# Loading four parameter arrays in 32-column pieces and turning them on VectorE, with a planner told of longer parameter loads

## The chip, the cores and the metric

One core of one Trainium2 chip runs the whole program. The metric is the device time of one execution in microseconds, the median of the runs taken. Engine names are those of the profile: PE is TensorE's matmul stream and PEld its weight loads, DVE is VectorE, ACT is ScalarE, POOL is GpSimd, SP is SyncE, which here only issues DMAs. Everything is float32; the two big matmuls of the MLP split each operand into a high and a low part and run in the `float32r` form.

## The reference

```python
xn = layernorm(u)                                  # u: 2048 tokens x 576 channels
dt = exp(log_dt)                                   # per channel
A  = -exp(log_A_real) + 1j * A_imag                # 576 x 128
C  = (C_real + 1j * C_imag) * dt[:, None]
K  = 2 * einsum("dn,dnl->dl", C, exp(A * dt[:, None] * pos)).real
y  = irfft(rfft(xn.T, 2L) * rfft(K, 2L))[:, :L].T  # a long convolution for each channel
s  = y + xn * D_skip
m  = gelu(layernorm(xn) @ w1 + b1) @ w2 + b2       # 576 -> 4608 -> 576, for each token
out = u + s * silu(m)
```

The four arrays of 576 x 128 that the change is about are `log_A_real`, `A_imag`, `C_real` and `C_imag`. The kernel wants them with the 128 modes on the partitions and the 576 channels along the free dimension, so each has to be transposed.

## The kernel before

**Two strands on one TensorE.** The MLP fills TensorE from start to end. It runs as 48 slots: two halves of the tokens, in each half 12 groups of 384 hidden units, and for each group two blocks of 512 tokens. A slot first makes three hidden tiles (`layer1`, L508: 14 matmuls of 512 columns each), then adds their products into four output tiles (`layer2`, L565: 72 matmuls of 288 columns). Between the two stand ACT (L541 gelu, L544 the high part `hh`) and DVE (L547, the low part `hl`). DVE also adds each finished output tile into `acc` (L573), and ACT and DVE split the next group's weights (L488, L485) as they arrive in the tile `raw` (L448, L450, L453, on SP's queue).

The convolution runs between the MLP's matmuls. Its parameters are prepared once (`params`, L664 to L776, the part that the change touches) and stored in DRAM in eight packs (`par_s`). For each of 36 blocks of 16 channels `tables` (L794) then loads a piece of them (`load_par`, L785, on POOL's queue, two buffers), makes sines and exponentials on DVE and ACT (first step L803 on DVE), and `kgen` (L872) multiplies them on TensorE (L885) into the convolution kernel. For each of six chunks of 96 channels `chunk` (L917) does the transforms: a forward stage (L958), a second stage (L996), the inverse (L1049) and a last stage (L1076), with DVE turning 32 x 32 blocks between them (L945, L1060). POOL stores the results (`s_s`, L1087). At half time the normalized tokens of the second half come back in pieces of 128 bytes (L1244) and DVE turns them (L1249).

**Who sets the order.** Every engine runs its instructions in the order in which they are written, and that order comes from a planner (`Order`, L55). It keeps a clock for each engine, gives each step a reckoned duration and, where it has one, a due time, and writes the step that can begin first. The strands are lists of steps; a step on `None` is a transfer: its loads are issued there, and what needs them is placed no sooner than its reckoned length later. The reckoned lengths of the convolution's TensorE stages are `X1, S2, INV, I1, KG` (L915). Two more numbers steer it: `END` (L1369), by which the stages of the chunks are spread over the run, and `ALONE` (L1370), how long a ready `kgen` waits for another convolution stage on which it can ride (`ride`, L896, then both are one interruption of the MLP) before it is written by itself.

**The parameters.** `loads` (L678) issues on SP's queue `log_dt`, and for each of the four arrays two DMAs, 512 rows and 64 rows, with 512 bytes to a packet. TensorE turns an array by four transposes of 128 x 128 and one of 64 x 128 (L692, L693) into PSUM (a pair of banks `cv`, which the convolution's stages use too), and ACT or DVE reads it from there. The tile names `kt`, `pr` and `mg` in the profile are the buffers of the raw arrays here: `kt` for `log_A_real` and `A_imag`, `pr` for `C_real`, `mg` for `C_imag`. The tile `U` holds `dt`. The rows behind these loads on SP's queue are the rest of the second group's `raw` weights (L450, L453), two small loads of `tvals` (L264), and eight loads of token rows (L346, tiles `w` and `v`), on which DVE takes the layer norm's statistics (L371).

Of the kernel before, what the change touches and what calls it, by code (L numbers as in the profile page):

```python
# [12 lines left out]
AF = mybir.ActivationFunctionType  # L13
OP = mybir.AluOpType
# [3 lines left out]
L, D, N, F = 2048, 576, 128, 4608  # L18
P = 128
# [3 lines left out]
CH = 96  # L23
# [10 lines left out]
PK = 72  # L34
# [4 lines left out]
TB = 512  # L39
# [168 lines left out]
def step(eng, dur, fn, need=(), mark=None, cv=0, at=0.0, late=0.0, tbl=None, by=1e9):  # L208
    return dict(eng=eng, dur=dur, fn=fn, need=tuple(need), mark=mark, cv=cv, at=at, late=late, tbl=tbl, by=by)
# [3 lines left out]
def mixer_kernel(ctx, tc, u, log_a_real, a_imag, c_real, c_imag, log_dt, d_skip, w1, b1, w2, b2,  # L213
                 f1, f2, g2, g1, tvals, ident, out, parts=("mlp", "s4d")):
    nc = tc.nc
# [34 lines left out]
    idt = ys_tile().rearrange("p i a b c -> p (i a b c)")[:, :P]  # L250
# [241 lines left out]
    turn = [0]  # L492
# [171 lines left out]
    def params():  # L664

        nrm, th, ph = (A2F[:, k * D:(k + 1) * D] for k in range(3))
        cr = sb.tile([P, NT, 48], F32, name="xc", bufs=NXC).rearrange("p a b -> p (a b)")[:, :D]
        out, early = [], []
        add = lambda *a, **k: out.append(step(*a, **k))
        src = (log_a_real, a_imag, c_real, c_imag)  # L670
        RP = []
        flat = lambda t: t.rearrange("p a b -> p (a b)")
        dt = UV[:, :D]
        PRM = [flat(sb.tile([P, 12, 64], F32, name="kt", bufs=2)) for _ in range(2)]
        PRM += [flat(sb.tile([P, 2, 4 * CH], F32, name="pr")), flat(sb.tile([P, SB, NM], F32, name="mg"))]
        T = [p[:, :D] for p in PRM] + [ys_tile().rearrange("p i a b c -> p (i a b c)")[:, :D]]

        def loads():  # L678
            nc.sync.dma_start(dt, dram(log_dt, 0, [[0, P], [1, D]]))
            for k, a in enumerate(src):  # L680
                r = PRM[k][:, :5 * N].rearrange("p (c n) -> p c n", c=5)
                nc.sync.dma_start(r[:, :4], a[:4 * P, :].rearrange("(c p) n -> p c n", p=P))
                nc.sync.dma_start(r[:64, 4], a[4 * P:, :])
                RP.append(r)
        add(None, 7.0, loads, at=20.0)
        add("ACT", act(D), lambda: nc.scalar.activation(dt, dt, AF.Exp), tbl="exp", late=0.0)
        Q = {}

        def turn(k):
            q = Q[k] = bank2("cv")  # L690
            for c in range(4):
                nc.tensor.transpose(q[:, 0, c * P:(c + 1) * P], RP[k][:, c], idt)  # L692
            nc.tensor.transpose(q[:, 1, :64], RP[k][:64, 4], idt[:64, :64])  # L693

        def both(k, f):
            f(slice(0, TB), Q[k][:, 0])
            f(slice(TB, D), Q[k][:, 1, :64])
        V, A = nc.vector, nc.scalar
        e, d = act(D) + 0.1, dve(D)
        turns = lambda k: add("PE", 0.8, lambda: turn(k), cv=1)  # L700
        add("PE", 0.8, lambda: turn(0), cv=1, need=[("x", 1)])
        add("ACT", e, lambda: both(0, lambda c, q: A.activation(nrm[:, c], q, AF.Exp)), cv=-1, tbl="exp", late=0.0,
            mark="nrm")
        turns(2)
        add("DVE", d + 0.1, lambda: both(2, lambda c, q: V.tensor_copy(cr[:, c], q)), cv=-1)
        turns(3)

        ci = ph  # L710
        add("DVE", d + 0.1, lambda: both(3, lambda c, q: V.tensor_copy(ci[:, c], q)), cv=-1)
# [10 lines left out]
        for h in H:  # L722
# [57 lines left out]
    def load_par(b):  # L780
        if b == NB:
            return
        PAR[b] = sb.tile([P, SB, NPAR], F32, name="par", bufs=2)

        nc.gpsimd.dma_start(PAR[b].rearrange("p (g i) k -> p g (i k)", g=4), dram(  # L785
            par_s, (b // 6 * CH + b % 6 * 4) * NPAR, [[D * NPAR, P], [24 * NPAR, 4], [1, 4 * NPAR]]))
# [7 lines left out]
    def tables(b):  # L794
# [3 lines left out]
        T = {}  # L798
# [32 lines left out]
        def weigh(k, part):  # L831
# [12 lines left out]
            else:  # L844
# [2 lines left out]

        n = SB * 32
        f = lambda g, *a: lambda: g(*a)
        return ([step(None, 3.0, lambda: load_par(b), mark=("par", b), need=[("pack", ((b // 6 + 1) * CH - 1) // PK)]  # L850
                      + ([("mags", b - 2)] if b > 1 else [("xn", k) for k in range(8, NT)])),
                 step("DVE", dve(SB * NV), f(phase, 0), need=[("wu", b - 2, 1)] if b > 1 else []),
                 step("DVE", dve(n), f(phase, 1)), step("ACT", act(SB * NV), whole),
# [6 lines left out]
                        need=[("sin", b, int(part < 2))] + ([("kg", b - 1)] if b else []),  # L860
# [704 lines left out]
```

## Time and profile before

| | us |
|---|---|
| median of 3 runs | 1088.73 |
| lowest and highest | 1088.65, 1090.24 |
| the profiled execution | 1090.13 |
| its span, first to last instruction | 1088.3 |
| PE busy in it | 1075.5 |
| DVE busy | 946.5 |
| ACT busy | 648.9 |
| granted TensorE clock | 0.999 |

A profiled execution's own time is its span and what lies around it, here 1.8 us more. PE's busy time is that of a pipeline: matmuls overlap, and a matmul that is shown with 0.29 us is followed by the next one after 0.13 us, so the starts of its rows tell more than their lengths. A wait in the table of waits is time in which the engine had nothing in its pipeline; the loss for the work behind it is some tenths more, since the pipeline also has to fill again.

### The profile page before, as it was taken

Reading aid. Unit: us, or ns where it says so; the run is one execution under the profiler, and the core shown is the slowest. Engines: PE = TensorE matmul, PEld = TensorE weight load, DVE = VectorE, ACT = ScalarE, POOL = GpSimd, SP = SyncE. Lnnn points to the kernel's source line nnn. Section 1 sums busy time; section 2 is a strip of 40 time slices with the busy share of each in tenths; the row PEclk is TensorE's granted clock in tenths of the full one; section 3 lists DMA queues with packets and bytes.
Section 4 is the critical chain, followed back from the end, with each engine's and each line's share of the span. In section 5 each row is a group of like instructions: output and inputs, shape, how many; then the busy total and the mean of one; then the engine's idle time right before and its main releaser. Section 6 shows DMA issues by size and latency. Waiting matters only on the chain.

```text
span 1088.3 us, 27217 instructions
## 1 busy us (share of the span) xinstructions
PE 1075.5 (99%) x11507; PEld 936.7 (86%) x11507; DVE 946.5 (87%) x1520; ACT 648.9 (60%) x972; POOL 197.3 (18%) x282
## 2 busy tenths in 40 slices
PE   9999999999999999999999999999999999999997
PEld 7889989888989788878888888888889888888896
DVE  7799688999999998989899999999988986767266
ACT  6666688667567565567756676666756443334233
POOL 5593622110000200010100110001000031110420
PEclk9999999999999999999999999999999999999999
DMA  8654557433251333424524232241314345341623
GB/s 241 235 163 168 199 213 187 134 99 113 59 118 43 94 99 69 109 59 103 132 99 117 50 101 70 69 106 49 99 41 128 65 141 168 99 148 47 223 73 88
DMA packets 129370, 125.55 MB, mean 115 GB/s; under 512 B 78820, under 2 KB 100912, under 8 KB 128224
## 3 DMA queue, kind: packets, MB, share of 16 engines
q1 hardware_dynamic: 113584, 76.44, 25.9%
q0 software_dynamic: 15104, 46.49, 13.9%
q8 instruction: 90, 1.47, 0.6%
q10 hardware_dynamic: 560, 0.89, 0.3%
q14 instruction: 32, 0.26, 0.1%
HBM read 95.52 MB, written 34.01 MB: 119 GB/s over the span
## 4 chain that ended last, share of the span: by engine, by line
PE 88%; DVE 7%; ACT 2%; DMA 2%; issue 1%; POOL 0%; DVEq 0%; ACTq 0%
PE mxa L508 19%; PE mxb L508 19%; PE mxb L565 19%; PE mxa L565 19%; PE cv L996 3%; PE cv L885 3%; PE cv L1049 2%; PE cv L958 1%; DVE acc L573 1%; DVE hl L547 1%; PE cv L1076 1%; DMA raw<-in_B_w_dram 1%; DVE A L945 1%; DVE w L803 0%; DMA idp<-in_ident_dram 0%
## 5 line engine op out<-in xcount | busy, mean ns | idle before, releaser
L565 PE MATMUL mxb<-w2h,hh 128*128 128x288 f32 x576 | 171.9, 298 | 2.0 <-DVE acc L573 2.0
L565 PE MATMUL mxa<-w2h,hh 128*128 128x288 f32 x573 | 170.9, 298 | 0.0
L565 PE MATMUL mxb<-w2h,hl 128*128 128x288 f32 x576 | 170.3, 296 | 0.5 <-DVE hl L547 0.5
L565 PE MATMUL mxa<-w2h,hl 128*128 128x288 f32 x573 | 169.1, 295 | 0.6 <-DVE hl L547 0.6
L565 PE MATMUL mxb<-w2l,hh 128*128 128x288 f32 x576 | 169.5, 294 | 0.0
L565 PE MATMUL mxa<-w2l,hh 128*128 128x288 f32 x573 | 168.7, 294 | 0.0
L547 DVE TENSOR_TENSOR hl<-h,hh 128x512 fp32r<-128x512 f32 x144 | 98.7, 686 | 71.4 <-ACT hh L544 70.9
L541 ACT ACTIVATE h<-mxa,b1t 128x512 f32<-128x512 f32 x73 | 50.2, 689 | 140.1 <-PE mxa L508 138.1
L785 POOL DMA_DIRECT2D par<-par_s x36 | 27.4, 762 | 525.5 <-DVE mg L828 523.9
L565 PEld LDWEIGHTS mxb<-w2h,hh 128*128 128x128 f32 x576 | 108.2, 188 | 10.5 <-issue 4.3
L565 PEld LDWEIGHTS mxa<-w2h,hh 128*128 128x128 f32 x573 | 107.6, 188 | 7.6 <-issue 3.0
L565 PEld LDWEIGHTS mxb<-w2h,hl 128*128 128x128 f32 x576 | 108.1, 188 | 1.2 <-DVE hl L547 1.1
L565 PEld LDWEIGHTS mxb<-w2l,hh 128*128 128x128 f32 x576 | 108.1, 188 | 0.6
L565 PEld LDWEIGHTS mxa<-w2h,hl 128*128 128x128 f32 x573 | 107.5, 188 | 0.8 <-DVE hl L547 0.8
L565 PEld LDWEIGHTS mxa<-w2l,hh 128*128 128x128 f32 x573 | 107.6, 188 | 0.6
L541 ACT ACTIVATE h<-mxb,b1t 128x512 f32<-128x512 f32 x71 | 48.9, 689 | 83.6 <-PE mxb L508 82.9
L544 ACT ACTIVATE hh<-h 128x512 fp32r<-128x512 f32 x144 | 90.9, 632 | 4.2
L573 DVE TENSOR_TENSOR acc<-mxb,acc 128x576 f32<-128x576 f32 x88 | 65.8, 748 | 16.1 <-PE mxb L565 16.0
L573 DVE TENSOR_TENSOR acc<-mxa,acc 128x576 f32<-128x576 f32 x88 | 65.3, 742 | 16.1 <-PE mxa L565 15.8
L508 PE MATMUL mxa<-XH,w1h 128*128 128x512 f32 x284 | 78.9, 399 | 0.2 <-DVE acc L573 0.2
L508 PE MATMUL mxb<-XH,w1h 128*128 128x512 f32 x280 | 78.0, 400 | 0.0
L488 ACT ACTIVATE w2h<-raw 128x576 fp32r<-128x576 f32 x72 | 44.3, 674 | 56.3 <-PE mxa L565 54.9
(240 smaller groups left out, 2464.5 us busy)
## 6 DMA issues: line engine op xcount, KB each, us to landing
raw<-in_B_w_dram SPq DMA_DIRECT2D x72, 288.0 KB, 3.2
raw<-in_B_w_dram SPq DMA_DIRECT2D x96, 192.0 KB, 3.1
par_s<-A POOLq DMA_DIRECT2D x8, 1080.0 KB, 5.4
par<-par_s POOLq DMA_DIRECT2D x36, 240.0 KB, 3.4
f2t<-f2q SPq DMA_DIRECT2D x24, 256.0 KB, 3.3
raw<-in_B_w_dram SPq DMA_DIRECT2D x48, 96.0 KB, 3.6
u_s<-in_A_u_dram POOLq DMA_DIRECT2D x16, 288.0 KB, 4.3
xc<-xn_s SPq DMA_DIRECT2D x48, 96.0 KB, 3.6
```

The source lines that it names most:

```text
L488: nc.scalar.activation(h, r, AF.Copy)
L508: nc.tensor.matmul(q, a, b, start=j == 0, stop=j == len(ops) - 1)
L541: nc.scalar.activation(t, q, AF.Gelu_apprx_tanh, bias=b1t[:, g * G + i:g * G + i + 1], scale=1.0)
L544: LAST[0] = nc.scalar.activation(hh[:, i], t, AF.Copy)
L547: nc.vector.tensor_sub(hl[:, i], t, hh[:, i].bitcast(F32))
L565: nc.tensor.matmul(q[:, dh, :288], a[:, i, c], b[:, i, d], start=i == 0 and k == 0, stop=i == G - 1 and k == 2)
L573: nc.vector.tensor_add(o, q[:, dh:dh + n, :288], b if g == 0 else o)
L785: nc.gpsimd.dma_start(PAR[b].rearrange("p (g i) k -> p g (i k)", g=4), dram(par_s, (b // 6 * CH + b % 6 * 4) * NPAR, [[D * NPAR, P], [24 * ...
L885: nc.tensor.matmul(q[32 * g:32 * g + 32, i // 2, i % 2 * 64:i % 2 * 64 + 64], U[:, ri, 4 * g + i, :], v[:, ri, 4 * g + i, :], start=ri == ...
L945: add("DVE", 0.5, lambda g=g, c0=c0: nc.vector.transpose(A2[:, :, x, c0:c0 + 12].rearrange("p k d r -> p d k r"), Q1ST[i, x][g // 2][:, g ...
L996: nc.tensor.matmul(Q[i][32 * q:32 * q + 32, f, 2 * ri:2 * ri + 2], m[r, 4 * i + q, 32 * ri:32 * ri + 32], A2[r, 4 * p + 2 * i + q // 2, :, ...
L1049: nc.tensor.matmul(QI[q // 2][64 * f:64 * f + 64, q % 2, i], MAT["g2t", p + i // 2][r, i % 2, ri], YS[p + i // 2][0][r, i % 2, ri, f], sta ...
```

## The change

The four arrays are loaded in sixteen DMAs. Each fills 32 partitions with 18 blocks of 32 x 32 numbers, so that a packet holds 32 numbers, 128 bytes. One 32 x 32 block transpose on DVE over 128 x 576 then turns a whole array in SBUF (`turns`). The transposes on TensorE are gone, with their PSUM banks; what read the turned arrays from PSUM now reads or updates them in SBUF, and the two copies L705 and L711 are replaced by the transposes themselves. The product with `dt` (L730 before) is one instruction on 576 columns instead of two. The arrays are loaded in the order 0, 2, 3, 1. The planner reckons 10 us instead of 7 for this step, 4.5 instead of 3 for each `load_par`, 1.97 instead of 2.05 for the inverse, and has `END` at 1000 instead of 1020 and `ALONE` at 6 instead of 4.

```diff
         def loads():
             nc.sync.dma_start(dt, dram(log_dt, 0, [[0, P], [1, D]]))
-            for k, a in enumerate(src):
-                r = PRM[k][:, :5 * N].rearrange("p (c n) -> p c n", c=5)
-                nc.sync.dma_start(r[:, :4], a[:4 * P, :].rearrange("(c p) n -> p c n", p=P))
-                nc.sync.dma_start(r[:64, 4], a[4 * P:, :])
-                RP.append(r)
-        add(None, 7.0, loads, at=20.0)
+            for k in (0, 2, 3, 1):
+                for q in range(4):
+                    nc.sync.dma_start(PRM[k][32 * q:32 * q + 32, :D].rearrange("p (b j) -> p b j", j=32), dram(
+                        src[k], 32 * q, [[N, 32], [32 * N, D // 32], [1, 32]]))
+        add(None, 10.0, loads, at=20.0)
...
-        def turn(k):
-            q = Q[k] = bank2("cv")
-            for c in range(4):
-                nc.tensor.transpose(q[:, 0, c * P:(c + 1) * P], RP[k][:, c], idt)
-            nc.tensor.transpose(q[:, 1, :64], RP[k][:64, 4], idt[:64, :64])
...
-        turns = lambda k: add("PE", 0.8, lambda: turn(k), cv=1)
-        add("PE", 0.8, lambda: turn(0), cv=1, need=[("x", 1)])
-        add("ACT", e, lambda: both(0, lambda c, q: A.activation(nrm[:, c], q, AF.Exp)), cv=-1, tbl="exp", late=0.0,
-            mark="nrm")
-        turns(2)
-        add("DVE", d + 0.1, lambda: both(2, lambda c, q: V.tensor_copy(cr[:, c], q)), cv=-1)
-        turns(3)
+        turns = lambda k, to, **a: add("DVE", d, lambda: V.transpose(to, T[k]), **a)
+        turns(0, nrm, need=[("x", 1)])
+        add("ACT", e, lambda: A.activation(nrm, nrm, AF.Exp), tbl="exp", late=0.0, mark="nrm")
+        turns(2, cr)
...
-        add("DVE", d + 0.1, lambda: both(3, lambda c, q: V.tensor_copy(ci[:, c], q)), cv=-1)
+        turns(3, ci)
...
-        turns(1)
-        add("DVE", d + 0.1, lambda: both(1, lambda c, q: V.scalar_tensor_tensor(
-            th[:, c], q, 1.0 / (2 * math.pi), dt[:, c], op0=OP.mult, op1=OP.mult)), cv=-1)
+        turns(1, th)
+        add("DVE", d, lambda: V.scalar_tensor_tensor(th, th, 1.0 / (2 * math.pi), dt, op0=OP.mult, op1=OP.mult))
...
-        return ([step(None, 3.0, lambda: load_par(b), mark=("par", b), need=[("pack", ((b // 6 + 1) * CH - 1) // PK)]
+        return ([step(None, 4.5, lambda: load_par(b), mark=("par", b), need=[("pack", ((b // 6 + 1) * CH - 1) // PK)]
...
-    X1, S2, INV, I1, KG = 1.08, 1.73, 2.05, 1.72, 1.1
+    X1, S2, INV, I1, KG = 1.08, 1.73, 1.97, 1.72, 1.1
...
-    END = 1020.0
-    ALONE = 4.0
+    END = 1000.0
+    ALONE = 6.0
```

Since the planner's numbers change, the order of nearly all later work changes with them, on every engine. Lines behind the change stand 17 lower in the new file (L1244 before is L1227 after, L1249 is L1232, L785 is L768, L803 is L786).

PE in the second slot: the first hidden tile ends in the bank `mxa`, the next begins in `mxb`. Before:

```order
L508 MATMUL mxa<-XR,w1r 128x512
L508 MATMUL mxa<-XR,w1s 128x512
L692 MATMUL cv<-ys,kt 128x128 x4
L693 MATMUL cv<-ys,kt 128x64
L508 MATMUL mxb<-XH,w1h 128x512 x4
L508 MATMUL mxb<-XL,w1h 128x512 x4
```

and in the changed kernel:

```order
L508 MATMUL mxa<-XR,w1r 128x512
L508 MATMUL mxa<-XR,w1s 128x512
L508 MATMUL mxb<-XH,w1h 128x512 x4
L508 MATMUL mxb<-XL,w1h 128x512 x4
L508 MATMUL mxb<-XH,w1l 128x512 x4
```

The five transposes of `log_A_real` are gone from between the two hidden tiles; the other three arrays' transposes go in the same way.

DVE at the same place, from the last split of the first half's tokens (`XR`) to the slot's third low part `hl`, in the changed kernel; before, no row stood between the `XR` row and the first `hl`:

```order
L425 TENSOR_TENSOR XR<-cv,XR 64x512
L687 STREAM_TRANSPOSE A_80<-kt 128x576
L687 STREAM_TRANSPOSE xc<-pr 128x576
L687 STREAM_TRANSPOSE A_80<-mg 128x576
L726 TENSOR_TENSOR A_80<-A_80,U 128x576
L371 BN_STATS st<-w 128x6
L547 TENSOR_TENSOR hl<-h_507,hh 128x512
L371 BN_STATS st<-w 128x6
L373 BN_AGGR U<-st 128x2
L371 BN_STATS st<-w 128x6
L547 TENSOR_TENSOR hl<-h_526,hh 128x512
L698 TENSOR_TENSOR kt<-kt,pr 128x576
```

Three transposes and the first statistics of a token row that comes by DMA (`w`) now stand ahead of the slot's first `hl`.

DVE before half time, behind the second chunk's stores of `s_s`, around the table step L803 that reads `par`. Before:

```order
L845 SCALAR_TENSOR_TENSOR v<-w,mg 128x16x32
L1249 STREAM_TRANSPOSE row<-row 128x512 x2
L945 STREAM_TRANSPOSE A_80<-cv 128x12x16x2 x4
L803 TENSOR_TENSOR w<-par,tv 128x1024
L547 TENSOR_TENSOR hl<-h_5686,hh 128x512
L806 TENSOR_TENSOR w<-w,par 128x16x32
L547 TENSOR_TENSOR hl<-h_5739,hh 128x512
```

and in the changed kernel, the table step behind the same stores (L786 is the old L803):

```order
L589 SCALAR_TENSOR_TENSOR acc<-h_6160,acc 128x288
L1232 STREAM_TRANSPOSE row<-row 128x512
L928 STREAM_TRANSPOSE A_80<-cv 128x12x16x2 x2
L953 TENSOR_TENSOR kt<-kt,dsk 128x12
L786 TENSOR_TENSOR w<-par,tv 128x1024
L547 TENSOR_TENSOR hl<-h_6154,hh 128x512
L789 TENSOR_TENSOR w<-w,par 128x16x32
```

Counted over the whole orders, the last stage of the second chunk (L1076 before, L1059 after), whose results those stores carry, follows the 63rd hidden tile before and the 67th after; the table step follows the 63rd `hl` before and the 69th after.

More of the change, by code (lines that the diff above doesn't have):

```diff
@@ L670, in params @@
         src = (log_a_real, a_imag, c_real, c_imag)
-        RP = []
         flat = lambda t: t.rearrange("p a b -> p (a b)")
@@ L679, in loads @@
             nc.sync.dma_start(dt, dram(log_dt, 0, [[0, P], [1, D]]))
-            for k, a in enumerate(src):
-                r = PRM[k][:, :5 * N].rearrange("p (c n) -> p c n", c=5)
-                nc.sync.dma_start(r[:, :4], a[:4 * P, :].rearrange("(c p) n -> p c n", p=P))
-                nc.sync.dma_start(r[:64, 4], a[4 * P:, :])
-                RP.append(r)
-        add(None, 7.0, loads, at=20.0)
-        add("ACT", act(D), lambda: nc.scalar.activation(dt, dt, AF.Exp), tbl="exp", late=0.0)
-        Q = {}
-        def turn(k):
-            q = Q[k] = bank2("cv")
-            for c in range(4):
[L692 to L697, printed above, removed]
+            for k in (0, 2, 3, 1):
[3 more added lines that the diff above has]
+        add(None, 10.0, loads, at=20.0)
+        add("ACT", act(D), lambda: nc.scalar.activation(dt, dt, AF.Exp), tbl="exp", late=0.0)
         V, A = nc.vector, nc.scalar
         e, d = act(D) + 0.1, dve(D)
-        turns = lambda k: add("PE", 0.8, lambda: turn(k), cv=1)
-        add("PE", 0.8, lambda: turn(0), cv=1, need=[("x", 1)])
-        add("ACT", e, lambda: both(0, lambda c, q: A.activation(nrm[:, c], q, AF.Exp)), cv=-1, tbl="exp", late=0.0,
-            mark="nrm")
-        turns(2)
-        add("DVE", d + 0.1, lambda: both(2, lambda c, q: V.tensor_copy(cr[:, c], q)), cv=-1)
-        turns(3)
+        turns = lambda k, to, **a: add("DVE", d, lambda: V.transpose(to, T[k]), **a)
+        turns(0, nrm, need=[("x", 1)])
+        add("ACT", e, lambda: A.activation(nrm, nrm, AF.Exp), tbl="exp", late=0.0, mark="nrm")
+        turns(2, cr)
         ci = ph
-        add("DVE", d + 0.1, lambda: both(3, lambda c, q: V.tensor_copy(ci[:, c], q)), cv=-1)
+        turns(3, ci)
         add("ACT", e, lambda: A.activation(T[0], cr, AF.Square))
```

## The prediction

> **What bounds the kernel now.** I read the page's busy times first, then the chain that ended last, then the table of waits for PE alone, and last the rows in time at each long wait.
>
> ```profile
> span 1088.3 us, 27217 instructions
> PE 1075.5 (99%) x11507; PEld 936.7 (86%) x11507; DVE 946.5 (87%) x1520; ACT 648.9 (60%) x972; POOL 197.3 (18%) x282
> PE 88%; DVE 7%; ACT 2%; DMA 2%; issue 1%; POOL 0%; DVEq 0%; ACTq 0%
> ```
>
> TensorE is busy for 99% of the span and carries 88% of the chain. So two things alone can change the time: what PE has to do, and the few places where it stands. The waits of PE, from an answer in which the rows of the start are left out:
>
> ```profile
> PE mxb L565 <- DVE acc L573: 2.0, 2, 1.5
> ...
> PE mxa L565 <- DVE hl L547: 0.6, 1, 0.6
> PE mxb L565 <- DVE hl L547: 0.5, 1, 0.5
> PE mxa L508 <- DVE acc L573: 0.2, 1, 0.2
> ```
>
> After the start PE stands five times, 3.3 us in all, each time for DVE. The two largest belong together; the rows of PE there, a matmul before and after each:
>
> ```profile
> 487.16 0.29 PE L565 MATMUL mxb<-w2l,hh 128*128 128x288 f32 x1
> 487.94 0.40 PE L565 MATMUL mxb<-w2h,hl 128*128 128x288 f32 x1 [0.49 <-DVE hl L547]
> ...
> 490.05 0.29 PE L565 MATMUL mxa<-w2h,hl 128*128 128x288 f32 x1
> 491.88 0.40 PE L565 MATMUL mxb<-w2h,hh 128*128 128x288 f32 x1 [1.54 <-DVE acc L573]
> ```
>
> An undisturbed L565 follows its forerunner by 0.13 us (the rows quoted under the first term show this). Here the steps are 0.78 and 1.83, so 0.65 and 1.70 us are lost, and 0.11 more each time because the next matmul then follows by 0.24: 2.6 us together. What made DVE late stands 6 us earlier:
>
> ```profile
> 477.10 1.93 DVE L945 STREAM_TRANSPOSE A<-cv 128x384 f32<-128x384 f32 x4
> 481.99 1.23 DVE L803 TENSOR_TENSOR w<-par,tv 128x1024 f32<-128x1024 f32 x1 [2.95 <-DMA par<-par_s]
> 483.13 0.69 DVE L547 TENSOR_TENSOR hl<-h,hh 128x512 fp32r<-128x512 f32 x1
> ```
>
> DVE stood 2.95 us for a parameter piece, with a low part `hl` of the MLP queued behind, and it had no room to catch up before PE asked for `acc`. The load went out late, behind the stores of a chunk on POOL's queue, and ran beside a burst of small pieces on SP's queue:
>
> ```profile
> 475.63 1.73 POOL L1087 DMA_DIRECT2D s_s<-ys  x3
> 477.36 0.78 POOL L785 DMA_DIRECT2D par<-par_s  x1
> 476.62 4.99 SPq L1244 DMA_DIRECT2D row<-y_s  x8
> ```
>
> Issued at 477.36, it was there 4.6 us later.
>
> **The change, term by term.** First, the transposes leave PE. One of the four, with its neighbours:
>
> ```profile
> 73.02 0.29 PE L565 MATMUL mxa<-w2h,hl 128*128 128x288 f32 x1
> 73.16 0.60 PE L692 MATMUL cv<-ys,kt 128*128 128x128 f32 x4
> 73.69 0.27 PE L693 MATMUL cv<-ys,kt 64*128 64x64 f32 x1
> 73.89 0.40 PE L565 MATMUL mxb<-w2h,hh 128*128 128x288 f32 x1
> 74.13 0.29 PE L565 MATMUL mxb<-w2l,hh 128*128 128x288 f32 x1
> 74.26 0.29 PE L565 MATMUL mxb<-w2h,hl 128*128 128x288 f32 x1
> ```
>
> From 73.02 to 74.13 are 1.11 us for two steps that would take 0.26, so one turn costs 0.85 us, and four cost **3.4 us**. All of it is on the path, since PE never rests there.
>
> Second, the riders. A `kgen` that stands alone interrupts the MLP by itself:
>
> ```profile
> 227.44 0.29 PE L565 MATMUL mxb<-w2h,hl 128*128 128x288 f32 x1
> 227.66 1.10 PE L885 MATMUL cv<-v,U 128*32 128x64 f32 x64
> 228.69 0.40 PE L565 MATMUL mxa<-w2h,hh 128*128 128x288 f32 x1
> 228.93 0.29 PE L565 MATMUL mxa<-w2l,hh 128*128 128x288 f32 x1
> ```
>
> Entering takes 0.22 instead of 0.13, and the second matmul behind it follows by 0.24 instead of 0.13: 0.2 us that a rider doesn't pay. In the two orders 14 of the 36 stand alone before and 12 after. That is **0.4 us**; I count 0.3, since a rider also lengthens its host's entry a little.
>
> Third, the wait for `par`. The order no longer puts the table step right behind the second chunk's stores: it now follows the 69th `hl`, with that chunk's last stage behind the 67th hidden tile, where before both numbers were 63. Two hidden tiles with what lies between are well over the 4.6 us that the load took. At the third and fourth set of stores that a `par` load follows, two and three low parts lie between as well, at the first most of a slot's second layer. So I take the wait to go, and with it **2.6 us**. Bounds: nothing, if something else is late next at that place (DVE is full there), and 2.6. What is late next is the rest of DVE's work before half time; the three small waits (536.9, 554.8 and 798.2 us) are left in the sum, as the same work is done in another order with as little room.
>
> Fourth, what the parameters cost now. SP issues sixteen loads instead of eight. The same form of load is in the trace, and so is the step on DVE:
>
> ```profile
> L1244 SPq DMA_DIRECT2D row<-y_s x36: 303/487/1305, 452.6 to 540.4; - x36
> L1249 DVE STREAM_TRANSPOSE row<-row x10: 665/697/708, 475.9 to 547.5; 128x512 f32<-128x512 f32 x8, 64x512 f32<-64x512 f32 x2
> ```
>
> A piece takes some 0.5 us to issue, a transpose of 512 columns 0.70; with 576 columns I estimate 0.75 (0.7 as the next one follows). On DVE four transposes replace two copies (L705, L711) and the halves of L730: work of the same size. On the queues the packets count. Two stretches of the DMA table, the first (480.5 to 483 us) nearly all packets of 128 bytes, the second (26 to 30 us) nearly all of 512:
>
> ```profile
> q1 hardware_dynamic: 2484, 0.31, 94.0%
> ...
> q1 hardware_dynamic: 1735, 0.86, 76.0%
> ```
>
> 2.5 us x 16 engines x 0.94 over 2484 packets are 15 ns for a packet; 4 x 16 x 0.76 over 1735 are 28 ns. The arrays were 2304 packets, 4.0 us of all engines; they become 9216, 8.7 us. By the table the engines are full at that time (76.0% and 29.8% of POOL's stores), so what is queued behind on SP comes up to 4.7 us later. The lower bound is SP's own time: sixteen issues of 0.5 are 8 us, from 21.07 to 28.36 it took 7.3, so at least 0.7 later. I take 4, nearer the upper end, as the engines were full. Behind them stand the rest of the second group's weights, `tvals`, and the token rows `w`:
>
> ```profile
> 21.07 0.51 SPq L682 DMA_DIRECT2D kt<-in_A_log_A_real_dram  x1
> ...
> 28.36 0.53 SPq L450 DMA_DIRECT2D raw<-in_B_w_dram  x1
> ...
> 30.87 1.07 SPq L264 DMA_DIRECT2D tv<-in_tvals_dram  x2
> 31.98 4.45 SPq L346 DMA_DIRECT2D w<-in_A_u_dram  x6
> ...
> w<-in_A_u_dram SPq DMA_DIRECT2D x1, 288.0 KB, 6.6
> ...
> 35.94 0.68 DVE L425 TENSOR_TENSOR XR<-cv,XR 64x512 fp32r<-64x512 f32 x1
> 39.60 0.69 DVE L547 TENSOR_TENSOR hl<-h,hh 128x512 fp32r<-128x512 f32 x1 [2.98 <-ACT hh L544]
> 40.21 0.81 DVE L371 BATCH_NORM_STATS2 st<-w 128x6 f32<-128x288 f32 x2
> ```
>
> The weights are split at 47 us and have 8 us to spare; `tvals` is used near 70. The first token row landed at 31.98 + 6.6 = 38.6 and would now land at 42.6. DVE gets to it sooner than before: from 36.6, three transposes, the product L726, at 39.5. So DVE stands there for 3 us, and now the slot's `hl` are behind. From 42.6: half the statistics 0.4, `hl` 0.6, the other half and the sum 0.65, the next row's 0.4, the second `hl` ends near 45.4; then L698 0.7, statistics 1.0, the third ends near 47.7. PE, two turns earlier than before (they stood at 38.02 and 45.23), starts its second layer at 44.3 and asks for the second `hl` six matmuls on, near 45.0, and for the third twenty on, near 47.0. It stands some **0.7 us**. With up to 3 us of delay it is nothing, with 4.7 it is 1.5.
>
> The Trainium skill, "DMA: Bandwidth & Descriptors", Specifications, gives 512 bytes as the least transfer for line rate, below which the engine reads, modifies and writes; this speaks against the change. The trace agrees in part: by the byte the small packets cost 2.1 times as much (15 ns for 128 bytes, 28 for 512), and that factor is already in the term.
>
> The other edits cost nothing by themselves: `INV`, `END`, `ALONE` and the 10 us only move work. The last stage of the last chunk stands behind the 133rd hidden tile of 144 (132nd before), so nothing of the convolution gets into the tail.
>
> Sum against the profiled execution: -3.4 - 0.3 - 2.6 + 0.7 = -5.6 us, so 1090.13 becomes 1084.5. That execution lay 1.4 above the median of the runs, so the median 1088.73 becomes **1083.1**, and I forecast 1083.2.
>
> **The rivals.** *The wait moves.* The whole order is new, and a DVE at 87% can be late at another place as easily; it may even be late at the old one. Then the 2.6 us don't come, or come back: 1085.7. For it: PE's five waits were all for DVE. Against it: 48 slots, and only one chain of waits over 1 us.
>
> *Two or three such places.* Each costs about 2.6; with the first term untouched, 1086.6 to 1091. For it: every due time that DVE missed here came from a transfer that was reckoned too short or from crowded work before half time, and the planner knows no more of these now, apart from `par`.
>
> *Slower: the small pieces run by the packet.* If a packet of 128 bytes cost what one of 512 costs there, 28 ns (no stretch of the trace has both sizes in a crowd), 9216 would be 16.1 us of all engines, a delay of 12.1 instead of 4. Each us beyond 4 is one more that DVE stands at the first token row and PE behind it: 0.7 + 8.1 = 8.8 us, and 1083.1 + 8.1 = 1091.2. From a delay of some 11.5 us on the kernel is slower by over 0.2%. Against it: the stretch that gave 15 ns was full too (94.0%).
>
> *The change doesn't do what it says:* the longer reckoned `par` moves no table step far enough. The order speaks against it at each set of stores; it would also give 1085.7, and I count it with the first rival.
>
> **How the numbers follow.** The forecast, 1081 to 1085, has a chance of 0.57; the wait that moves, 0.17; two or three such places, 0.15; the slow packets, or more than three new waits, 0.11. Within 0.2% (2.2 us), about what a measurement of this kernel can tell from no change, means 1086.6 to 1090.9. The first two cases are faster by more than that: 0.74. The third is the same: 0.15. The fourth is slower: 0.11. For 8 times in 10 the range takes the first two cases and half the third: 1080.8, where every wait after the start is gone and the first token row costs nothing, to 1088.6.
>
> **What would show it.** In the changed profile: PE's matmuls go from the first hidden tile of the second slot to the second without a gap, and no L692 or L693 rows are left. Between 39 and 43 us DVE waits for `w` from DRAM, 3 us if the delay is 4, and PE stands under 1 us at 45 to 47.5. No DVE step waits for `par` by more than 1 us. PE's waits after the start sum to 2 us or less; each us more is one more in the time. The prediction is wrong if that sum is over 4, or if the first token row lands after 46 us.

## The result, and the profile after

The changed kernel takes 1092.32 us, the median of 13 runs (1091.1 to 1094.38), beside 1089.11 us for the kernel before on the same chip (13 runs). The ratio is 1.0026, with a 95% interval of 1.0017 to 1.0034: slower by about a quarter of a per cent, where 1083.2 us and a gain were forecast. The profiled execution took 1091.50 us. Its page begins with these lines, and the third is the chain that ended last:

```profile
span 1089.7 us, 27199 instructions
PE 1073.3 (98%) x11487; PEld 934.4 (86%) x11487; DVE 946.0 (87%) x1519; ACT 650.8 (60%) x972; POOL 200.8 (18%) x282
PE 90%; POOL 2%; DVE 1%; DMA 1%; issue 1%; SPq 1%; ACT 1%; ACTq 0%; POOLq 0%; DVEq 0%
```

PE does 2.2 us less work than before and the span is 1.4 us longer, so PE has nothing in its pipeline for about 3.6 us more. A name is new in the chain: SPq, the issuing of DMAs. PE's waits in the changed kernel, with three rows of the start left out:

```profile
PE mxb L508 <- ACT h L541: 4.5, 1, 4.5
PE mxa L565 <- DVE hl L547: 1.4, 1, 1.4
...
PE mxb L565 <- DVE hl L547: 1.0, 1, 1.0
```

All five waits of before are gone. Three others stand in their place, and the largest is for ACT, for which PE, once past the start, never waited in the kernel before. Here is PE at that place (columns: start, length, then the instruction, and in brackets the idle time ahead of it and who ended it):

```profile
178.82 0.39 PE L508 MATMUL mxa<-XR,w1s 128*128 128x512 f32 x1
183.72 1.77 PE L508 MATMUL mxb<-XH,w1h 128*128 128x512 f32 x4 [4.51 <-ACT h L541]
185.29 1.91 PE L508 MATMUL mxb<-XL,w1h 128*128 128x512 f32 x4
187.00 1.33 PE L508 MATMUL mxb<-XH,w1l 128*128 128x512 f32 x4
188.17 0.39 PE L508 MATMUL mxb<-XR,w1r 128*128 128x512 f32 x1
```

Two losses can be read off. Between 178.82 and 183.72 are 4.9 us for a step of 0.23, so 4.7 us are lost in the stand. Then the twelve matmuls that the rows from 183.72 to 187.00 hold take until 188.17, that is 4.45 us, where twelve steps of 0.23 are 2.7: 1.8 us more. The table of stretches says why (length, busy time of PE, PEld, DVE, ACT and POOL, then the granted clock, the share of the DMA engines and GB/s):

```profile
183.70:187.50 3.80, 3.77 (x10) 2.96 (x11) 3.80 (x5) 1.84 (x3) 2.51 (x6) 0.55 0.26 73
```

TensorE's clock was granted at 0.55 in these 3.8 us behind the stand: it stood at one half from 184.1 to 187.5 us, for 3.4 us, and at 1 before and after. So this one place costs 6.5 us, more than the whole forecast gain of 5.6.

Now back along the chain, from PE to ACT, in the same kernel:

```profile
179.72 0.68 ACT L488 ACTIVATE w2h<-raw 128x576 fp32r<-128x576 f32 x1 [5.57 <-DMA raw<-in_B_w_dram]
180.31 1.04 ACT L798 ACTIVATE w<-w 128x1024 f32<-128x1024 f32 x1
181.25 0.42 ACT L290 ACTIVATE g2t<-f2t 128x256 f32<-128x256 f32 x1
181.69 1.28 ACT L541 ACT_TABLE_LOAD   x1
182.99 0.69 ACT L541 ACTIVATE h<-mxb,b1t 128x512 f32<-128x512 f32 x1
```

ACT stood 5.57 us for the third piece of the next group's second weights (`raw`), of which it has to make the high part (L488). The gelu that empties the bank `mxb` was queued behind, after two other steps and a table load. PE may not write `mxb` again before that gelu has read it. And the piece was late because of what SP issued ahead of it:

```profile
166.40 0.81 SPq L448 DMA_DIRECT2D raw<-in_B_w_dram  x2
167.51 8.48 SPq L911 DMA_DIRECT2D xc<-xn_s  x8
176.10 0.60 SPq L448 DMA_DIRECT2D raw<-in_B_w_dram  x1
```

The eight loads of the first chunk's input (`xc`, L911, L928 before) stand between the second and the third weight piece. SP needs 8.48 us to issue them, so the third piece left at 176.10, 9.7 us behind the first two. In the kernel before, the three pieces stood together, the six pieces of the next first weights followed, and `xc` came behind all of them:

```profile
165.45 2.39 SPq L448 DMA_DIRECT2D raw<-in_B_w_dram  x3
175.66 2.21 SPq L450 DMA_DIRECT2D raw<-in_B_w_dram  x4
177.92 1.11 SPq L453 DMA_DIRECT2D raw<-in_B_w_dram  x2
179.33 10.94 SPq L928 DMA_DIRECT2D xc<-xn_s  x8
```

So what differs here is the order of SP's queue, 170 us into the run, long after the four arrays of the change were loaded.

The early part of the run went as forecast in kind, but cost more. DVE, around the first token row:

```profile
43.49 0.46 DVE L371 BATCH_NORM_STATS2 st<-w 128x6 f32<-128x288 f32 x1 [4.28 <-DMA w<-in_A_u_dram]
43.87 0.68 DVE L547 TENSOR_TENSOR hl<-h,hh 128x512 fp32r<-128x512 f32 x1
```

DVE stood 4.28 us for the token row where 3 were reckoned, and the row was there at 43.5 instead of 42.6. PE behind it:

```profile
46.30 0.40 PE L565 MATMUL mxb<-w2h,hl 128*128 128x288 f32 x1 [1.03 <-DVE hl L547]
```

This is the largest of three stands there. They lose 1.9 us together (summed over the steps between the matmuls from 44.3 to 48.7 us, each against its undisturbed 0.13), where 0.7 was forecast.

The third wait, at 145 us, is a small copy of the wait for `par` that the change was to remove. DVE there:

```profile
143.64 2.33 DVE L738 TENSOR_TENSOR A<-A 128x1008 f32<-128x1008 f32 x2 [2.16 <-DMA par_s<-A]
```

DVE waits for the buffer of a parameter pack whose store (`par_s`) is still running, with a low part `hl` behind that begins at 145.89, and PE loses 1.7 us. Behind this stand, of 1.45 us by the trace, the clock stayed at 1.

### The profile page after: what moved, and what is told of

Same layout as the page of the kernel before. It is cut to its first block, busy times and chain, and to the rows that moved or that the text cites. A ratio compares the mean times of both kernels' runs of the same rounds, so it can differ in the third digit from the quotient of the medians.

```text
span 1089.7 us, 27199 instructions
## 1 busy us (share of the span) xinstructions
PE 1073.3 (98%) x11487; PEld 934.4 (86%) x11487; DVE 946.0 (87%) x1519; ACT 650.8 (60%) x972; POOL 200.8 (18%) x282
## 4 chain that ended last, share of the span: by engine, by line
PE 90%; POOL 2%; DVE 1%; DMA 1%; issue 1%; SPq 1%; ACT 1%; ACTq 0%; POOLq 0%; DVEq 0%
PE mxb L565 20%; PE mxa L565 20%; PE mxb L508 20%; PE mxa L508 19%; PE cv L868 3%; PE cv L979 3%; PE cv L1032 2%; PE cv L941 2%; PE cv L1059 1%; SPq L911 1%; POOL w L395 1%; POOL v L395 1%; DMA par_s<-A 1%; DMA raw<-in_B_w_dram 0%; DVE A L644 0%
## 5 line engine op out<-in xcount | busy, mean ns | idle before, releaser
L565 PE MATMUL mxb<-w2h,hl 128*128 128x288 f32 x576 | 170.6, 296 | 1.2 <-DVE hl L547 1.0
L565 PE MATMUL mxb<-w2h,hh 128*128 128x288 f32 x576 | 171.3, 297 | 0.0
L565 PE MATMUL mxa<-w2h,hl 128*128 128x288 f32 x573 | 169.3, 296 | 1.4 <-DVE hl L547 1.4
L565 PE MATMUL mxa<-w2h,hh 128*128 128x288 f32 x573 | 170.5, 298 | 0.0
L565 PE MATMUL mxb<-w2l,hh 128*128 128x288 f32 x576 | 169.5, 294 | 0.0
L565 PE MATMUL mxa<-w2l,hh 128*128 128x288 f32 x573 | 168.6, 294 | 0.0
L768 POOL DMA_DIRECT2D par<-par_s x36 | 27.5, 763 | 491.9 <-DVE mg L811 474.0
L565 PEld LDWEIGHTS mxa<-w2h,hh 128*128 128x128 f32 x573 | 107.6, 188 | 8.4 <-issue 4.1
L565 PEld LDWEIGHTS mxb<-w2h,hh 128*128 128x128 f32 x576 | 108.2, 188 | 6.6 <-issue 2.4
L565 PEld LDWEIGHTS mxb<-w2h,hl 128*128 128x128 f32 x576 | 108.1, 188 | 2.3 <-DVE hl L547 2.1
L565 PEld LDWEIGHTS mxa<-w2h,hl 128*128 128x128 f32 x573 | 107.5, 188 | 1.9 <-DVE hl L547 1.9
L565 PEld LDWEIGHTS mxb<-w2l,hh 128*128 128x128 f32 x576 | 108.2, 188 | 0.6
L565 PEld LDWEIGHTS mxa<-w2l,hh 128*128 128x128 f32 x573 | 107.6, 188 | 0.6
L488 ACT ACTIVATE w2h<-raw 128x576 fp32r<-128x576 f32 x72 | 44.4, 674 | 68.2 <-PE mxa L565 62.5
L508 PE MATMUL mxa<-XL,w1h 128*128 128x512 f32 x284 | 76.2, 390 | 0.0
```

Of the source, the lines that this page charges most:

```text
L488: nc.scalar.activation(h, r, AF.Copy)
L508: nc.tensor.matmul(q, a, b, start=j == 0, stop=j == len(ops) - 1)
L565: nc.tensor.matmul(q[:, dh, :288], a[:, i, c], b[:, i, d], start=i == 0 and k == 0, stop=i == G - 1 and k == 2)
```

## The experiments

The main theory, **A**: the loss is the place of the `xc` loads on SP's queue. The main rival, **B**: the new order as a whole, or the planner's numbers, or the small loads, made the loss, and the stand at 178.8 us is only where it shows.

### `xc_behind`: the same order, `xc` behind the three weight pieces

The loads of the first chunk are held back until SP has issued the third piece; every other engine's rows stay as they are in the changed kernel.

```diff
             for _ in range(NEXT[which - 1][i]):
                 load_raw()
+            if which == 1 and i == KB and PEND:
+                PEND.pop()()
...
-        def load():
+        def load(now=c > 0):
+            if not now:
+                PEND.append(lambda: load(True))
+                return
             XC[0] = sb.tile([P, 2, 32, 24], F32, name="xc", bufs=NXC)
```

> The changed kernel, with one thing put back: the first chunk's eight loads of token rows (xc) are issued on SP behind the next group's weight loads raw instead of between the second and the third of them; every other row on every engine stands where it stood. Theory A (SP's queue: the third weight piece is issued 9 us late, ACT stands for it with the next gelu queued behind, PE stands 4.9 us and then runs at about half clock for 4 us): the wait at 179 us and the low clock go, about 6.4 us less than the changed kernel, a ratio to the kernel before near 0.996, mean clock 0.999. Rival B (the DMA engines are crowded there and the piece would be late anyway): ACT still waits over 2 us for raw and the ratio stays at 1.001 or more. Rival C (the loss is spread over the new order, and the wait at 179 only took slack that other waits would have taken): PE's other waits grow, the ratio is 0.999 to 1.003.

Measured: 1085.36 us (5 runs), ratio to the kernel before 0.9968 (0.9956 to 0.998); below the changed kernel by 7.0 us by the medians, 6.3 by the two ratios, where 6.4 were expected. SP's and then PE's rows that answer to those of the changed kernel:

```profile
166.87 2.39 SPq L448 DMA_DIRECT2D raw<-in_B_w_dram  x3
169.55 8.36 SPq L917 DMA_DIRECT2D xc<-xn_s  x8
```

```profile
PE mxa L568 <- DVE hl L550: 1.6, 1, 1.6
...
PE mxb L568 <- DVE hl L550: 1.2, 2, 1.0
```

The wait for ACT is gone and the two waits for DVE are left as they were. The eight loads still take 8.4 us, now where nobody waits for what is behind them. As no other engine's order differs, theory A is shown: without this place the loss against the kernel before is gone, and a gain of 0.3% stands there instead.

### `xc_half`: four of the eight loads ahead of the third piece, four behind

```diff
+            some(range(4) if c else (0, 1))
+            if not c:
+                PEND.append(lambda: some((2, 3)))
```

> The changed kernel with four of the eight xc loads ahead of the third weight piece and four behind the weights, nothing else moved. Theory A: half of SP's 8.5 us is left ahead, the piece is issued some 4 us sooner, PE stands about 0.5 to 1.5 us instead of 4.9, and the clock stays full (a stand of 1.7 us in the changed kernel had no low clock behind it): ratio to before 0.996 to 0.998. Rival B (crowded DMA): as in the changed kernel, 1.002 to 1.003. If the low clock follows any stand of PE, some us at about half clock stand behind this one too and the ratio is 0.998 to 0.999.

Measured: 1090.03 us (12 runs, widely spread from 1086.08 to 1094.78), ratio 1.0005 (0.9994 to 1.0016), between the two others. This lies above what I had expected by theory A (0.996 to 0.998, or up to 0.999 with a low clock) and below rival B. Half the loads ahead cost about half the stand, where 0.5 to 1.5 us were expected: SP issued the third piece 4.3 us sooner than it would have behind all eight, and PE still stood for 2.35 us. SP's and PE's rows, from an execution of 1091.38 us:

```profile
169.05 4.12 SPq L917 DMA_DIRECT2D xc<-xn_s  x4
173.28 0.58 SPq L448 DMA_DIRECT2D raw<-in_B_w_dram  x1
173.91 5.22 SPq L917 DMA_DIRECT2D xc<-xn_s  x4
```

```profile
183.10 2.07 PE L511 MATMUL mxb<-XH,w1h 128*128 128x512 f32 x4 [2.35 <-ACT h L544]
```

The third piece left at 173.28, and ACT, which waited for it, began its split at 179.09, 5.8 us later. In the changed kernel these are 176.10 and 179.72, 3.6 us. Here four more loads of `xc` left SP right behind the piece; that they slowed its landing fits, but was not tried apart. The stand is half as long and the low clock behind it is not: the stretch from 183.10 to 186.90 had a clock of 0.56 here as well.

```profile
183.10:186.90 3.80, 3.80 (x10) 3.04 (x11) 3.80 (x5) 1.82 (x3) 2.50 (x6) 0.56 0.54 191
```

### `xc_between_before`: the kernel before, with `xc` put between two weight pieces

```diff
             for _ in range(NEXT[which - 1][i]):
+                if which == 1 and i == KB and PEND:
+                    PEND.pop()()
                 load_raw()
```

> The kernel before with the fault put in: the first chunk's eight xc loads are issued between the second and the third weight piece of the next group, near 206 us, nothing else moved; they also come some 25 us later than they did, so the first chunk's own forward stage on xc (near 215 us) may wait for them. Theory A: ACT waits about 5 us for the third raw piece, PE stands 4 to 5 us for a gelu near 215, low clock behind it, 5 to 8 us more in all: ratio 1.005 to 1.008, with up to 3 us more where PE waits for xc. Rival B or C (the place of the xc loads does not matter): ratio 0.999 to 1.002.

Measured: 1096.72 us (5 runs), ratio 1.0068 (1.0055 to 1.0081). The size is that of a large loss, but PE did not stand where I had meant it to. In the kernel before the second and third piece of the group in question came late enough that `xc` itself was now overdue, and PE waited for that in the forward stage (L964, which is L958 before):

```profile
214.53 1.57 PE L964 MATMUL cv<-xc,f1t 32*64 32x384 f32 x6
217.26 0.88 PE L964 MATMUL cv<-xc,f1t 32*64 32x384 f32 x8 [1.16 <-DMA xc<-xn_s]
218.60 1.54 PE L964 MATMUL cv<-xc,f1t 32*64 32x384 f32 x2 [0.46 <-DMA xc<-xn_s]
220.07 2.08 PE L511 MATMUL mxb<-XH,w1h 128*128 128x512 f32 x4
```

The stage took 5.5 us, where it takes 0.83 in the kernel before:

```profile
214.71 0.90 PE L958 MATMUL cv<-xc,f1t 32*64 32x384 f32 x16
215.54 1.19 PE L508 MATMUL mxb<-XH,w1h 128*128 128x512 f32 x4
```

These 4.7 us, and what a spell of low clock took behind them (2.4 us by the steps of L511), make up nearly all of the 7.5 us. The clock was at one half from 218.1 to 225.0 us, so it fell within the stage. So the run shows once more what eight loads at a wrong place on SP's queue cost. It does not show that weights held back by them cost as much in that order, which is what it was for.

### `tv_later`: `tvals` behind the token rows

```diff
-    tl["steps"].append(step(None, 4.0, load_tv, at=30.0))
+    tl["steps"].append(step(None, 4.0, load_tv, at=45.0))
```

> The changed kernel with the two loads of tvals moved on SP from ahead of the eight token row loads (w, v) to behind them, nothing else moved. Theory A (the first token row is late because it is queued behind the sixteen small loads and then behind the two tvals loads, which run 5 us while the engines are nearly idle): the first w lands near 39.5 instead of 43.5, DVE's wait for it falls from 4.3 to under 1 us, PE's stands at 44 to 48.5 us (1.9 us in all) go: 1.5 to 2 us less than the changed kernel, ratio to before near 1.001. Rival: the row is late because the small packets fill the engines; then tvals only change place and DVE still waits 3 us or more.

Measured: 1091.25 us (11 runs), ratio 1.0018 (1.001 to 1.0027). DVE's wait for the token row fell from 4.28 to 1.27 us:

```profile
40.43 0.46 DVE L371 BATCH_NORM_STATS2 st<-w 128x6 f32<-128x288 f32 x1 [1.27 <-DMA w<-in_A_u_dram]
```

PE's early stands went with it, 1.9 us of them, but the time fell by only 1.1, where 1.5 to 2 were expected. PE's largest wait says where some of it went:

```profile
182.18 2.07 PE L508 MATMUL mxb<-XH,w1h 128*128 128x512 f32 x4 [4.90 <-ACT h L541]
```

The stand for the gelu grew from 4.5 to 4.9 us: PE arrives earlier at a place whose end is set by SP and not by PE. The low clock there lasted longer too: it was at one half from 179.7 to 186.5 us, so that the twelve matmuls behind the stand lost 2.1 us instead of 1.8. Time won ahead of a wait on another chain is partly waited away there.

### `numbers_only` and `turns_only`: the two halves of the change

The first is the kernel before with `par` at 4.5, `INV` 1.97, `END` 1000 and `ALONE` 6; the second is the changed kernel with those four as they were.

```diff
-        return ([step(None, 3.0, lambda: load_par(b), mark=("par", b), need=[("pack", ((b // 6 + 1) * CH - 1) // PK)]
+        return ([step(None, 4.5, lambda: load_par(b), mark=("par", b), need=[("pack", ((b // 6 + 1) * CH - 1) // PK)]
...
-    X1, S2, INV, I1, KG = 1.08, 1.73, 2.05, 1.72, 1.1
+    X1, S2, INV, I1, KG = 1.08, 1.73, 1.97, 1.72, 1.1
...
-    END = 1020.0
-    ALONE = 4.0
+    END = 1000.0
+    ALONE = 6.0
```

> This is the kernel before with the four numbers of the planner alone (4.5 us for each load of par, INV 1.97, END 1000, ALONE 6); loads of 512 bytes and TensorE's turns stay. On SP's queue the three w2 pieces of a group then stand together, with the first chunk's eight xc loads ahead of all three, and not between the second and the third. Theory A (the loss of the whole change is the xc loads that came between two weight pieces, which only the turns' edit and the numbers together bring about): no stand of PE near 178 to 190 us and no low clock there; the wait for par is gone (-2.6 us), so 1086 to 1087.5 us, ratio 0.997 to 0.999; if TensorE also stands at a late store of a parameter pack near 145 us as in the changed kernel (1.7 us), 1088, ratio 0.999. Theory B (the planner's numbers by themselves make an order that is worse, wherever xc stands): 1090 us or more, ratio above 1.001.

> This is the changed kernel with the four numbers of the planner as they were before (3.0, 2.05, 1020, 4); the sixteen small loads, the transposes on DVE and the 10 us stay. On SP's queue the eight xc loads again stand between the second and the third w2 piece. Theory A (that place is the loss): PE stands 4 to 5 us for the gelu near 178 us and runs at a clock near 0.55 for 3 to 4 us behind it, 6.5 us in all; the first token row costs 1.9 us; the wait for par before half time may be there again (2.6 us) or not: 1091.5 to 1095 us, ratio 1.002 to 1.005. Theory B (the planner's numbers made the loss): no such stand, and 1089.1 - 3.4 + 1.9 = 1087.6 us, ratio below 0.9995.

Measured for the numbers alone: 1085.63 us (5 runs), ratio 0.996 (0.9948 to 0.9973), a little better than theory A had it. After the start PE stands nowhere; these are all its waits:

```profile
PE cv L413 <- DVE st L371: 1.5, 1, 1.5
PE mxa L1131 <- POOL XL L1125: 1.3, 1, 1.3
PE cv L413 <- DVE row L386: 0.2, 1, 0.2
```

All five waits of the kernel before are gone, not only the two for `par`, and none came instead; rival B falls as far as the numbers go. On SP's queue the weights come first, and the `xc` loads (L928) behind them:

```profile
166.51 2.39 SPq L448 DMA_DIRECT2D raw<-in_B_w_dram  x3
...
178.99 10.62 SPq L928 DMA_DIRECT2D xc<-xn_s  x8
```

Measured for the turns alone: 1094.77 us (5 runs), ratio 1.0047 (1.0033 to 1.0061). The total is within what theory A expected, the way to it is not. `xc` stands between the pieces again, and ACT waits 4.22 us for the third one:

```profile
183.42 0.69 ACT L488 ACTIVATE w2h<-raw 128x576 fp32r<-128x576 f32 x1 [4.22 <-DMA raw<-in_B_w_dram]
```

But PE stands 1.6 us behind it and not 4.5 (1.29 at a `kgen` and 0.28 within it), and the clock stays up there. ACT's wait is 1.35 us shorter than in the changed kernel, its work between the split and the gelu 0.3 us shorter, and in this order PE has a `kgen` to do, some 1.3 us, before it needs the bank again:

```profile
185.55 0.32 PE L868 MATMUL cv<-v,U 128*32 128x64 f32 x8 [1.29 <-DVE v L826]
```

The rest is made of smaller waits for DVE, of which PE's table has 5.4 us in six stands (`hl` and `acc`). Three of them, 3.1 us, are at the token row and at the late store, as in the changed kernel. Behind the two at the token row, of 0.48 and 1.05 us, the clock fell here: it was at one half from 48.7 to 52.1 us, and fourteen steps of L565 took 3.35 us instead of 1.85. Another stand, of 1.0 us at 168.8 us, lies behind the longer of two waits for `par` on DVE, which the changed kernel doesn't have:

```profile
DVE w L786 <- DMA par<-par_s: 2.5, 2, 2.2
```

So the two halves pull apart: the planner's numbers gain 0.4%, and loading and turning the arrays in the new way loses 0.5% by itself, although it takes work off PE. The stands that were traced back (token row, late store, `par`, weights) all begin with a transfer that comes late; the two others, of 0.5 and 0.8 us, are not followed back here.

### `behind_tv` and `behind_tv_pack`: the changed kernel, mended

The first has the edits of `xc_behind` and `tv_later` together; the second also reckons a longer store of a parameter pack:

```diff
-            stored.append(step(None, 6.0, lambda: None, mark=("pack", i), need=[("send", i)]))
+            stored.append(step(None, 8.5, lambda: None, mark=("pack", i), need=[("send", i)]))
```

> The changed kernel with both repairs: the first chunk's xc loads behind the three w2 pieces, and the two loads of tvals behind the token rows. Theory A: the stand near 178 us and the low clock behind it stay away, so that the 1.9 us at the first token row, which the later tvals alone did not bring to the end of the run, are now gained in full: 1083.3 to 1084 us, ratio 0.994 to 0.996, 1.5 to 2 us under the xc repair alone. Rival: DVE's early work is late for something else than the token row, and the gain is given back at the next tight place (145 us, late pack store): 1085.3, ratio 0.9965, as with the xc repair alone.

> The same with the store of a parameter pack reckoned at 8.5 us instead of 6 by the planner (it took 5.8 and 7.1 us on POOL's queue in the changed kernel). If the stand of PE near 145 us comes from the low part hl queued behind a DVE step that waits for that store, it goes, 1.7 us: 1081.6 to 1082.5 us, ratio 0.993 to 0.994. Rival: the later order of the packs makes another wait of about the same size later, so no change against the run with both repairs, or up to 1.5 us slower than that.

Measured: 1083.57 us (5 runs), ratio 0.9948 (0.9935 to 0.996), and 1082.29 us (5 runs), ratio 0.9935 (0.9922 to 0.9947). Both as expected. With the wait for weights away, the later `tvals` take 0.2% off the ratio, where they took 0.08% off the changed kernel's; the longer store takes away the wait at 145 us, and the median is 1.3 us lower, though the two intervals overlap. All of PE's waits in the last version, both at the start:

```profile
PE cv L413 <- DMA idp<-in_ident_dram: 2.4, 1, 2.4
PE mxa L1120 <- POOL XL L1114: 1.3, 1, 1.3
```

This is the fastest version, 10 us below the changed kernel and 7 below the one before. It and `numbers_only` are the two kernels in which PE stands nowhere after the start. PE's work differs in them by the four turns, and the time by 3.3 us in the medians and 2.7 in the traced spans; the forecast had the turns at 3.4. Their orders differ too, so this is a fit and not a clean measurement.

## Why the prediction was wrong

**Right: the turns.** 3.4 us were forecast for the four transposes. In the changed kernel PE goes from the first hidden tile of the second slot to the second without a gap:

```profile
37.60 0.39 PE L508 MATMUL mxa<-XR,w1s 128*128 128x512 f32 x1
37.83 1.07 PE L508 MATMUL mxb<-XH,w1h 128*128 128x512 f32 x4
```

and the pair above gives 2.7 to 3.3. **Not measured apart: the riders**, 0.3 us.

**Right in effect, the reason not shown: the wait for `par`.** The wait at half time is gone, as forecast. But the longer reckoned `par` was not needed for that: in `turns_only`, where `par` is reckoned at 3 us, PE does not stand after 194.0 us either. What the longer reckoning may have removed is the wait for `par` at 166 us, which that run has and the kernel before had not. So that the old wait went was in part luck: it went in every new order that was run. The other small waits, which the sum left in, went too; this part of the change did better than forecast (4.1 us with `numbers_only`, where 2.6 and 0.3 were forecast).

**Right in kind, too small: the token row.** It came 0.9 us later than reckoned, and PE lost 1.9 us instead of 0.7. The delay was put at 4 us between bounds of 0.7 and 4.7; the row landed 4.9 us later, 4.6 of it already at the issue (36.59 us instead of 31.98), and the price at the upper end, 1.5, was nearest. The rival of the slow packets, with a delay of 12.1 us, is ruled out by the same rows. The two loads of `tvals`, which stand ahead of the token rows before and after, hold them up by 3 us (`tv_later`). They are in the rows that the prediction quotes, and it counted them only as something that is needed late.

**Wrong: the step that priced moved work at nothing.** "`INV`, `END`, `ALONE` and the 10 us only move work", and of the parameters' own loads only what was queued behind them within the next 12 us was followed. The order had been followed on PE and DVE, the engines that had waited before, and the place of `xc` on SP's queue had not. There the turns' edit moved eight loads ahead of one weight piece, which cost 4.7 us of standing and 1.8 us of low clock. Of the rivals, "two or three such places" comes nearest, as there are three new stands, but its range ended at 1091, each place was priced like the wait removed, 2.6 us, and PE's waits for DVE pointed to the wrong engine for the largest. That the run came out slower was covered only by the last chance, 0.11, for slow packets or more than three new waits, neither of which came. The price of this stand was not that of the last wait seen: it was the later issue of the weight piece (8.7 us), less the slack behind it (8.7 us for 4.7 us of stand, so 4.0 of slack). `xc_half` agrees if the landing is counted too: 4.2 us of later issue and 2.2 of slower landing, less 4.0, are 2.4 us, where 2.35 was measured.

The prediction's own test came out against it: PE's waits after the start sum to 6.9 us, over the 4 from which on it called itself wrong. Corrected, the sum against the profiled execution is: -3.4 for the turns, -0.3 for the riders, -4.8 for all waits of before with their refilling (2.6 had been counted), +1.9 at the token row, +1.7 at the late store, +4.7 and +1.8 at the weights, +1.6 in all; the span grew by 1.4. The riders' term stands in it as forecast. Between the two medians it is 3.2 us: the traced execution before lay 1.0 above the median of its 13 runs, the one after 0.8 below. The granted clock over the 13 runs of the changed kernel goes from 0.993 to 0.998 and is lowest in the slowest, so a low clock that lasts longer in some executions, as in the trace of `tv_later`, may be the rest; this is not shown, since only one execution of it was traced.

With the `xc` loads alone put back behind the weights, the changed kernel runs at 1085.36 us, in the predicted range of 1080.8 to 1088.6. Most of the forecast's error, 6.5 us of the 9.1, is that one queue; the token row was priced too low by 1.2, the late store (1.7) was not in the sum, and the waits that went were worth 2.2 more than counted.

**Still open.** `turns_only` has more small waits than the theory gives it; the kernel before has others, and which of the four numbers takes each of them away was not tried. The price of held-back weights in the kernel before's own order was not isolated either, since the run meant for it made PE wait for `xc` instead.

## What to carry to other kernels

When an order is written anew, compare the queues that only issue transfers as closely as the engines that compute, and for each block of loads that jumped ahead of another transfer multiply its issues by their measured length, and hold that, with what it may add to the landing, against the slack of the one behind. A gain ahead of a tight place on another chain is partly waited away there, so mend the tight places first and measure small gains last, or together. An engine that waits for a transfer hands its lateness to everything queued behind it: in the changed kernel it was a gelu behind a weight split, and a low part behind a token row's statistics or a parameter step, that stopped the bottleneck, not the late data itself.

## What was not expected of the hardware

A stand of TensorE can have a second price. Behind a stand of 4.51 us the clock was 0.55 for 3.8 us (1.8 us lost), behind one of 2.35 us 0.56 for as long (1.7 us lost), and behind stands of 1.45 us (the changed kernel at 145 us), 1.54 us (the kernel before at 491.9 us) and 1.70 us (`xc_half` at 148.2 us) it did not fall. But the longest gap alone does not decide it. In `turns_only` the clock fell at 48.7 us behind two stands of 0.48 and 1.05 us that lay 1.7 us apart, and in `xc_between_before` it fell within a stage in which the matmuls came in three bursts over 5.5 us, though no single gap was over 1.16 us. In the traces of this case a spell at half clock within the run lasts 3.4 us (`turns_only`, `xc_half`, the changed kernel) or 6.8 us (`tv_later`, `xc_between_before`). The Trainium skill, "TensorE: Matmul & The Clock Gate", Part 1, has the clock halved after an idle window of about 3.4 us. The half clock agrees; the 2.35 us stand and the two stands of `turns_only` are shorter than that window and lost the clock all the same, and here the measurement decides.

Issuing is dear: eight `xc` loads kept SP busy for 8.4 to 8.5 us in the changed kernel and in `xc_behind`, about 1.05 us each, and for 7.4 to 10.9 us in the other runs in which they stand together, while the two weight loads ahead of them in the changed kernel took 0.4 us each. The time that an issue takes is not fixed: the four weight loads (L450) behind `xc` took 4.74 us there and 2.21 in the kernel before. In the changed kernel the two loads of `tvals`, 16 KB each, took 6.0 and 6.5 us from issue to landing, and with them behind the token rows DVE waited 3 us less, of which 1.1 us is the earlier issue.
